# Quest-style attention and a capacity-limited expert layer: keys and queries loaded as token-major rows of 256 B, and turned, reduced and cast in thirds

## The chip, the core and the metric

The kernel runs on one core of one Trainium2 chip. Its time is the device time of one execution in microseconds (us). A core has five engines that run side by side, each through its own instructions in order: TensorE (PE in the profile, its weight loads PEld), VectorE (DVE), ScalarE (ACT), GpSimd (POOL), and SyncE (SP), which here only issues DMA transfers. A name with a q at its end (SPq, POOLq) is the part of an engine that issues transfers and waits.

## What is computed

```python
q, k, v: (4, 8, 768, 64)                     # batch, heads, tokens, width; float32
k_chunks = k.reshape(B, H, 24, 32, D)        # 24 chunks of 32 tokens
k_min, k_max = np.min(k_chunks, axis=3), np.max(k_chunks, axis=3)
ub = np.sum(np.maximum(q * k_min, q * k_max), axis=-1)     # bound per query and chunk
ub = np.where(causal, ub, -1e9)
top_chunks = np.argsort(ub, axis=-1)[..., -6:]             # the 6 best chunks per query
scores = scale * np.matmul(q, k.transpose(0, 1, 3, 2))     # masked to these and to the causal part
attn_out = softmax(scores) @ v
x = attn_out.transpose(0, 2, 1, 3).reshape(3072, 512)      # then the expert layer
logits = x @ w_gate; expert_idx = argmax(logits); gate_w = probability of that expert
# per expert the 80 tokens with the largest gate_w:
out[tok_idx] = gate_w[tok_idx, None] * (np.maximum(x[tok_idx] @ w1[e], 0) @ w2[e])
```

## The kernel before

The 32 pairs of batch and head are taken as 8 quads of 4 heads. On the 128 partitions lie 4 heads by 32. A quad has three query blocks of 256 tokens (THIRD = 256), and these have 1, 2 and 3 pairs of key blocks, so a quad is 6 rounds and the attention is 48 rounds, in the loop at lines 815 to 883 (rd is the round, g its quad, r its place in the quad).

For a quad, `load_k` and `load_q` (line 218) bring 768 KB each into one buffer each, kn and qn: partition (head, t) holds 24 rows of 64 floats. With the view of lines 186 and 187 the token is 24 t + c, so the 24 rows of a partition lie one behind another in memory, 6 KB. `load_v` (line 232) is four loads of 192 KB, whose rows are 64 floats, 256 B.

`prep(g)` (line 239) takes the tiles of a quad and returns its steps. K (line 256): VectorE turns blocks of 32 x 32 from kn to kT (line 253; in quad 0 in two halves, else in one instruction of 1536 columns), GpSimd casts kT to KB, VectorE takes the minimum and the maximum of each chunk (lines 261, 262), GpSimd subtracts them (line 263). Q (line 266): VectorE turns qn to qT, ScalarE takes relu into qp, GpSimd casts to QB. `bound` (line 276) is 80 small matmuls into ps_u, which takes the four banks that the scores use too; VectorE turns them into ub (line 295), and the banks are free again. `rank` and `unselect` make the mask from ub. kT, qT, qp, ub, kn and qn have one buffer each, so the next quad's data can come in only when the last reader is done.

A round is: scores on TensorE (`score`), exponentials on ScalarE (line 358, tile E), a causal cut on GpSimd for some (line 362), and one round later `value` and `denom` on TensorE. After a query block, `scales` and `rows` normalize: TensorE transposes into a pool of two banks (ps_dT, ps_xn), VectorE makes den, rec, lg_h (lines 421 to 428) and x_nat (line 443). After the second quad of a batch (odd g) `gates` follows: a chain on VectorE with lg, mx, sh (line 462), an exponential ex on ScalarE (line 465), and gmask (line 488). `merge` (line 510) turns gmask on TensorE (ps_g, line 515), ScalarE copies it to cand, and VectorE alternates MAX8 and MATCH_REPLACE8 on it (lines 522, 524) to keep the 80 best per expert. After the rounds come the gathers and the experts' two matmuls.

The order on TensorE and SP is the order of the program (line 799). On VectorE, ScalarE and GpSimd a planner puts the instructions in order before the run, by its own costs and by due times that it works out backwards from the users; on the chip each engine keeps that order. In the loop, the K step of quad g+1 stands at r = 0 of quad g, the Q step at r = 1, `bound` behind the values of r = 3; the loads of quad g+2 stand at r = 3, behind the v loads of r = 1 and in front of zero fills of the output (line 131) and stores of x (line 449) in SP's queue. Since K and Q wait only for their data and buffers, the planner puts them up to a quad ahead. Weights come by GpSimd's queue (line 145).

Of the kernel before, what the change touches and what calls it, by code (L numbers as in the profile page):

```python
# [35 lines left out]
def kernel(  # L36
# [146 lines left out]
    slotrhs = big.tile([P, TBLK, 6, NEXP], BF16, name="slotrhs")  # L183
    cand = [big.tile([P, CAP + SEQ], F32, name=f"cand_{s}") for s in range(2)]

    q4 = q.rearrange("b h (t c) d -> (b h t) c d", t=CHUNK)
    k4 = k.rearrange("b h (t c) d -> (b h t) c d", t=CHUNK)
    v4 = v.rearrange("b h (c p) d -> p (b h c) d", p=P)
    x_dram_v = x_dram.rearrange("(c p) d -> p c d", p=P)

# [8 lines left out]
    with tc.tile_pool(name="small", bufs=2) as small, \  # L199
# [18 lines left out]
        def load(g, src, name, parts=1):  # L218
            dst = qkp.tile([P, NCHUNK, HEAD_D], F32, name=name)
            n = NCHUNK // parts  # L220
            for i in range(parts):
                nc.sync.dma_start(out=dst[:, n * i:n * (i + 1), :],
                                  in_=src[P * g:P * (g + 1), n * i:n * (i + 1), :])
            nats[(g, name)] = dst

        def load_k(g, parts=1):
            load(g, k4, "kn", parts)
# [8 lines left out]
                                  in_=v4[:, 24 * g + 6 * h:24 * g + 6 * (h + 1), :])  # L236
            nats[(g, "vn")] = dst

        def prep(g, parts=1):
            s = g % 2  # L240
            qn, kn = nats[(g, "qn")], nats[(g, "kn")]
            kT = qfp.tile([P, 2, SEQ], F32, name="kT")
            qT = qfp.tile([P, 2, SEQ], F32, name="qT")
            qp = qfp.tile([P, 2, SEQ - P], F32, name="qp")
            kmx = small.tile([P, 2, NCHUNK], F32, name="kmx")
            spare["kT"], spare["qT"], spare["qp"] = kT[:], qT[:], qp[:]

            def turn(dst, src):
                n = NCHUNK // parts
                view = dst[:].rearrange("p f (t c) -> p c f t", c=NCHUNK)  # L250
                for i in range(parts):
                    cs = slice(n * i, n * (i + 1))
                    nc.vector.transpose(out=view[:, cs],  # L253
                                        in_=src[:, cs, :].rearrange("p c (f d) -> p c f d", f=2))

            def keys():
                turn(kT, kn)
                nc.gpsimd.tensor_copy(out=KB[s][:], in_=kT[:])
                kv = kT[:].rearrange("p f (c t) -> p f c t", t=CHUNK)
                lo = KMM[s][:, 0, :, 0:NCHUNK]  # L260
                nc.vector.tensor_reduce(out=lo, in_=kv, axis=mybir.AxisListType.X, op=ALU.min)
                nc.vector.tensor_reduce(out=kmx[:], in_=kv, axis=mybir.AxisListType.X, op=ALU.max)  # L262
                nc.gpsimd.tensor_tensor(out=KMM[s][:, 1, :, 0:NCHUNK], in0=kmx[:], in1=lo,  # L263
                                        op=ALU.subtract)

            def queries():
                turn(qT, qn)
                nc.scalar.activation(out=qp[:], in_=qT[:, :, P:SEQ],  # L268
                                     func=mybir.ActivationFunctionType.Relu)
                nc.gpsimd.tensor_copy(out=QB[s][:], in_=qT[:])  # L270

            ub = rankp.tile([P, 5, 4, 32], F32, name="ub")
            top8 = rankp.tile([P, 5, 4, 8], F32, name="top8")
            spare["ub"], spare["top8"] = ub[:], top8[:]

            def bound():
                ps_u = [psS.tile([P, 5, 32], F32, space=bass.MemoryType.PSUM, tag="ps_S",
                                 name="ps_u") for _ in range(4)]
                part = lambda x, lo: x[:, lo:].rearrange("p (i j t) -> p i j t", i=5, t=32)
                for w in range(3):  # L280
                    for f in range(1 if w == 0 else 2):
                        for j in range(4):
                            for h in range(4):
                                rs = slice(32 * h, 32 * (h + 1))
                                if w == 0:
                                    lhsT, rhs = later[rs, :], part(ind, P)
                                elif w == 1:
                                    lhsT, rhs = KMM[s][rs, 0, f, :], part(qT[:, f, :], P)
                                else:
                                    lhsT, rhs = KMM[s][rs, 1, f, :], part(qp[:, f, :], 0)  # L290
                                nc.tensor.matmul(out=ps_u[h][32 * j:32 * (j + 1), :, :], lhsT=lhsT,  # L291
                                                 rhs=rhs[rs, :, j, :], start=(w == 0),
                                                 stop=(w == 2 and f == 1), skip_group_check=True)
                for h in range(4):
                    nc.vector.transpose(out=ub[:, :, h, :], in_=ps_u[h][:])  # L295

            def rank():
                for j in range(5):
                    for h in range(4):
                        nc.vector.max(out=top8[:, j, h, :], in_=ub[:, j, h, 0:NCHUNK])  # L300
                nc.vector.tensor_tensor(out=PEN[s][:, :, :, 0:NCHUNK], in0=ub[:, :, :, 0:NCHUNK],
                                        in1=top8[:, :, :, 5:6].to_broadcast([P, 5, 4, NCHUNK]),
                                        op=ALU.is_lt)

            def unselect():
                ps_pen = misc([P, 5 * P], BF16, "ps_pen")
                for j in range(5):
                    nc.tensor.transpose(ps_pen[:, j * P:(j + 1) * P],
                                        PEN[s][:, j].rearrange("p h c -> p (h c)"), ident_bf[:])
                nc.scalar.activation(out=PENT[s][:], in_=ps_pen[:],  # L310
                                     func=mybir.ActivationFunctionType.Copy)

            return {"K": keys, "Q": queries, "bound": bound, "rank": rank, "unselect": unselect}

        rounds = []
        for g in range(NQUAD):
# [480 lines left out]
        stages = 0  # L797
        FREEZE = N - 6
        with tc.manual_schedule(engines={mybir.EngineType.PE, mybir.EngineType.SP}):
            load_k(0, 2)  # L800
            load_q(0, 2)
            nc.sync.dma_start(out=wg_sb[:], in_=moe_w_gate.rearrange("(t r) e -> r t e", r=P))
            load_v(0)
            load_k(1)
            load_q(1)
            load_v(1)
            u = prep(0, 2)
            for step in ("K", "Q", "bound", "rank", "unselect"):
                u[step]()
            nc.vector.memset(cand[0][0:NEXP, 0:CAP], 0.0)  # L810
            build_projection()
            build_selection()
# [2 lines left out]
            for rd in range(N + 1):  # L815
                g, r = divmod(rd, 6)
                before, after = [], []
                if r == 0 and g + 1 < NQUAD:
                    u = prep(g + 1)
                if rd - 4 in ends:  # L820
                    before.append(lambda e=ends[rd - 4]: rows(*e))
                if rd - 3 in ends:
                    before.append(lambda e=ends[rd - 3]: scales(*e))
                if g + 1 < NQUAD:
                    if r == 0:
                        before.append(u["K"])
                    elif r == 1:
                        before.append(u["Q"])
                    elif r == 4:
                        before.insert(0, u["rank"])  # L830
                    elif r == 5:
# [155 lines left out]
```

## Time and profile before

| what | value |
|---|---|
| two runs | 424.32 and 422.92 us, median 423.62 us |
| profiled execution | 419.83 us, of which 418.0 us from the first to the last instruction (the span) |
| TensorE busy (matmuls) | 280.4 us (67%) |
| VectorE busy | 255.8 us (61%) |
| ScalarE busy | 143.6 us (34%) |
| GpSimd busy | 124.9 us (30%) |
| mean granted TensorE clock | 0.846 of full speed |

A busy share is a mean over stages with different limits. Which engine sets the end of a stage is read from the waits and the timeline of that stage. A wait names the instruction that waited and the one that came last of those it waited for. The granted clock has two levels, 1.2 GHz (0.50 of full speed) and 2.4 GHz (1.00); a number between is a mean.

### The profile page before, as it was taken

To read this page: it belongs to the slowest core of one execution; us is meant where nothing else is said; L and a number is where in the kernel's file an instruction comes from. 1 tells how busy PE (TensorE), PEld (TensorE's weight loads), DVE (VectorE), ACT (ScalarE), POOL (GpSimd) and SP (SyncE) were. 2 spreads that over 40 slices of the span, in tenths; PEclk is the share of its full clock that TensorE was granted. 3 is DMA by queue.
4 is the path that set the end of the run, shared out by engine and by line. 5 is a ranking of instruction groups with operands and counts; after the bars stand their busy time and mean duration, and the time that the engine had idled before them with its cause. 6 is when DMAs were issued, how large, how long until landed. Compare 5 with 4: busy or idle time off the path is not lost. (4 is left out here: it accounts for less than half of the span.)

```text
span 418.0 us, 12461 instructions
## 1 busy us (share of the span) xinstructions
PE 280.4 (67%) x5330; PEld 173.1 (41%) x5330; DVE 255.8 (61%) x686; ACT 143.6 (34%) x322; POOL 124.9 (30%) x289
## 2 busy tenths in 40 slices
PE   0319799189735896399383990897579988435882
PEld 0214565055423453255151550554346644233661
DVE  6996630874279974781499928759893672621331
ACT  1116364045501362236222450454224452601220
POOL 3633061026400231216301510363315320151221
PEclk9957999769968699589977997699689998755997
DMA  9542019463993079175990291719748900011111
GB/s 238 172 120 78 4 26 262 145 101 104 234 245 129 2 133 286 29 162 115 290 225 4 30 243 60 104 46 182 115 91 155 176 29 27 25 39 26 48 34 40
DMA packets 48328, 47.82 MB, mean 114 GB/s; under 512 B 26918, under 2 KB 38310, under 8 KB 48272
## 3 DMA queue, kind: packets, MB, share of 16 engines
q0 software_dynamic: 13536, 18.67, 26.5%
q1 hardware_dynamic: 34736, 28.35, 23.1%
q8 instruction: 42, 0.69, 0.7%
q14 instruction: 14, 0.11, 0.1%
HBM read 53.10 MB, written 10.76 MB: 153 GB/s over the span
## 5 line engine op out<-in xcount | busy, mean ns | idle before, releaser
L358 ACT ACTIVATE E<-ps_S 128x384 f32<-128x384 f32 (+1 forms) x192 | 88.9, 547 | 67.0 <-PE ps_S L351 65.9
L375 PE MATMUL ps_num<-E,vn 128*32 128x256 f32 (+1 forms) x1536 | 99.2, 378 | 0.0
L362 POOL TENSOR_SCALAR_AFFINE_SELECT E<-E 128x256 f32<-128x256 f32 x96 | 40.6, 446 | 109.8 <-ACT E L358 109.8
L375 PEld LDWEIGHTS ps_num<-E,vn 128*32 128x32 f32 x1536 | 52.4, 116 | 32.8 <-issue 9.6
L391 PE MATMUL ps_den<-E,ones 128*32 128x256 f32 (+1 forms) x768 | 54.1, 370 | 5.9 <-ACT DSB L409 5.9
L347 PE MATMUL ps_S<-QB,KB 32*128 32x256 bf16 (+1 forms) x768 | 42.0, 276 | 21.0 <-DVE ub L295 17.1
L253 DVE STREAM_TRANSPOSE kT<-kn 128x1536 f32<-128x1536 f32 (+1 forms) x9 | 32.1, 3589 | 32.5 <-DMA kn<-in_k_dram 32.5
L253 DVE STREAM_TRANSPOSE qT<-qn 128x1536 f32<-128x1536 f32 (+1 forms) x9 | 32.1, 3569 | 11.5 <-PE ps_u L291 8.9
L291 PE MATMUL ps_u<-ind,later 32*32 32x160 bf16 x128 | 6.0, 270 | 46.7 <-ACT E L358 32.2
L391 PEld LDWEIGHTS ps_den<-E,ones 128*32 128x32 f32 x768 | 25.8, 114 | 24.7 <-ACT DSB L409 10.9
L522 DVE MAX8 cand<-cand 8x8 f32<-8x848 f32 (+2 forms) x40 | 33.2, 830 | 4.5 <-ACT cand L516 3.8
L347 PEld LDWEIGHTS <-KB 32*128 32x128 bf16 x768 | 20.3, 97 | 36.2 <-issue 32.2
L421 DVE TENSOR_REDUCE den<-ps_dT 128x4 f32<-128x8 f32 x48 | 5.8, 155 | 43.9 <-PE ps_dT L417 43.9
L268 ACT ACTIVATE qp<-qT 128x1280 f32<-128x1280 f32 x8 | 10.2, 1270 | 57.5 <-DVE qT L253 46.2
L524 DVE MATCH_REPLACE8 cand<-cand,cand 8x848 f32<-8x848 f32 (+2 forms) x36 | 29.4, 818 | 0.0
L351 PE MATMUL ps_S<-PENT,ind 32*128 32x256 bf16 (+1 forms) x384 | 27.1, 271 | 0.4 <-ACT PENT L310 0.2
L443 DVE TENSOR_TENSOR x_nat<-ps_xn,rec 128x512 bf16<-128x512 f32 x24 | 16.2, 675 | 15.1 <-PE ps_xn L442 15.1
L465 ACT ACTIVATE ex<-sh 128x16 f32<-128x16 f32 x12 | 2.6, 215 | 60.6 <-DVE sh L462 60.6
L291 PEld LDWEIGHTS <-later 32*32 32x32 bf16 x128 | 2.4, 91 | 50.5 <-issue 36.2
L263 POOL TENSOR_TENSOR KMM<-kmx,KMM 128x48 f32<-128x48 f32 x8 | 2.6, 326 | 59.7 <-DVE kmx L262 59.7
L398 ACT ACTIVATE npt<-ps_num 128x512 f32<-128x512 f32 x24 | 14.7, 614 | 9.5 <-PE ps_num L375 9.5
L515 PE MATMUL ps_g<-ident_f,gmask 128*8 128x128 f32 x18 | 3.7, 314 | 21.2 <-DVE gmask L488 20.5
(208 smaller groups left out, 450.5 us busy)
## 6 DMA issues: line engine op xcount, KB each, us to landing
w<-in_moe_w_dram POOLq DMA_DIRECT2D x11, 1024.0 KB, 9.5
vn<-in_v_dram SPq DMA_DIRECT2D x32, 192.0 KB, 7.2
out_dram<-zero_tile SPq DMA_DIRECT2D x12, 512.0 KB, 6.9
kn<-in_k_dram SPq DMA_DIRECT2D x7, 768.0 KB, 6.5
qn<-in_q_dram SPq DMA_DIRECT2D x7, 768.0 KB, 6.9
x_dram<-x_nat SPq DMA_DIRECT2D x12, 257.0 KB, 2.9
kn<-in_k_dram SPq DMA_DIRECT2D x2, 384.0 KB, 3.5
qn<-in_q_dram SPq DMA_DIRECT2D x2, 384.0 KB, 4.9
```

The source lines that it names most:

```text
L253: nc.vector.transpose(out=view[:, cs], in_=src[:, cs, :].rearrange("p c (f d) -> p c f d", f=2))
L268: nc.scalar.activation(out=qp[:], in_=qT[:, :, P:SEQ], func=mybir.ActivationFunctionType.Relu)
L347: nc.tensor.matmul(out=ps_S[h][:, m, 0:wid], lhsT=KB[s][rs, w, keys], rhs=QB[s][rs, w, q0:q0 + wid], start=(w == 0), stop=False, skip_grou ...
L351: nc.tensor.matmul(out=ps_S[h][:, m, lo - q0:wid], lhsT=ind[rs, keys], rhs=PENT[s][rs, lo - P:q0 + wid - P], start=False, stop=True, skip_ ...
L358: nc.scalar.activation(out=E[:].rearrange("p m q -> p (m q)")[:, 0:last], in_=ps_S[h][:].rearrange("p m q -> p (m q)")[:, 0:last], func=my ...
L362: nc.gpsimd.affine_select(out=E[:, :, 0:P], in_=E[:, :, 0:P], compare_op=ALU.is_ge, fill=0.0, base=0, pattern=[[0, 2], [1, P]], channel_mu ...
L375: nc.tensor.matmul(out=NUM[q0:q0 + 32, a, c0:THIRD], lhsT=nats[(g, "vn")][:, kb, 2 * a + r, 32 * f:32 * (f + 1)], rhs=Es[rd][2 * a + r][:, ...
L391: nc.tensor.matmul(out=dn[q0:q0 + 32, c0:THIRD], lhsT=ones32[:, a, :], rhs=Es[rd][2 * a + r][:, m, 0:wid], start=(i == 0 and x == 0), stop ...
L398: nc.scalar.activation(out=npt[:], in_=NUM[:], func=mybir.ActivationFunctionType.Copy)
L443: nc.vector.tensor_tensor(out=xbuf[(b, t)][:, :, P * gi:P * (gi + 1)].bitcast(BF16).rearrange("p j (k d) -> p j k d", d=HEAD_D), in0=ps_xn ...
L522: nc.vector.max(out=top, in_=src[:, 0:w])
L524: nc.vector.match_replace(out=src[:, 0:w], in_to_replace=top, in_values=src[:, 0:w], imm_value=-2.0)
```

## The change

Keys and queries are loaded so that partition (head, t) holds token 32 c + t: rows of 64 floats, 256 B, that lie 8 KB apart in memory. A load is now one per head, onto 32 partitions; in quad 0 each is also cut into three by chunks, so keys and queries of quad 0 are 24 loads instead of 4, those of every other quad 8 instead of 2. The turn writes rows of 32 floats side by side (before, each float of such a row lay 24 floats from the last). Turn, cast, the two extremes, the subtraction and relu work on a third (8 chunks, 256 tokens) at a time; K and Q are now lists of three steps. `prep(g+2)` is called at r = 5 of quad g, one round sooner; its steps stand where they stood.

```diff
-    q4 = q.rearrange("b h (t c) d -> (b h t) c d", t=CHUNK)
-    k4 = k.rearrange("b h (t c) d -> (b h t) c d", t=CHUNK)
+    q4 = q.rearrange("b h (c t) d -> (b h) t c d", t=CHUNK)
+    k4 = k.rearrange("b h (c t) d -> (b h) t c d", t=CHUNK)
...
             for i in range(parts):
-                nc.sync.dma_start(out=dst[:, n * i:n * (i + 1), :],
-                                  in_=src[P * g:P * (g + 1), n * i:n * (i + 1), :])
+                for h in range(4):
+                    nc.sync.dma_start(out=dst[32 * h:32 * (h + 1), n * i:n * (i + 1), :],
+                                      in_=src[4 * g + h, :, n * i:n * (i + 1), :])
...
-            def turn(dst, src):
-                n = NCHUNK // parts
-                view = dst[:].rearrange("p f (t c) -> p c f t", c=NCHUNK)
-                for i in range(parts):
-                    cs = slice(n * i, n * (i + 1))
-                    nc.vector.transpose(out=view[:, cs],
-                                        in_=src[:, cs, :].rearrange("p c (f d) -> p c f d", f=2))
-
-            def keys():
-                turn(kT, kn)
-                nc.gpsimd.tensor_copy(out=KB[s][:], in_=kT[:])
-                kv = kT[:].rearrange("p f (c t) -> p f c t", t=CHUNK)
-                lo = KMM[s][:, 0, :, 0:NCHUNK]
+            def turn(dst, src, i):
+                cs, ts = slice(8 * i, 8 * (i + 1)), slice(THIRD * i, THIRD * (i + 1))
+                nc.vector.transpose(
+                    out=dst[:, :, ts].rearrange("p f (c t) -> p c f t", t=CHUNK),
+                    in_=src[:, cs, :].rearrange("p c (f d) -> p c f d", f=2))
+                return cs, ts
+
+            def keys(i):
+                cs, ts = turn(kT, kn, i)
+                nc.gpsimd.tensor_copy(out=KB[s][:, :, ts], in_=kT[:, :, ts])
+                kv = kT[:, :, ts].rearrange("p f (c t) -> p f c t", t=CHUNK)
+                lo = KMM[s][:, 0, :, cs]
                 nc.vector.tensor_reduce(out=lo, in_=kv, axis=mybir.AxisListType.X, op=ALU.min)
-                nc.vector.tensor_reduce(out=kmx[:], in_=kv, axis=mybir.AxisListType.X, op=ALU.max)
-                nc.gpsimd.tensor_tensor(out=KMM[s][:, 1, :, 0:NCHUNK], in0=kmx[:], in1=lo,
+                nc.vector.tensor_reduce(out=kmx[:, :, cs], in_=kv, axis=mybir.AxisListType.X,
+                                        op=ALU.max)
+                nc.gpsimd.tensor_tensor(out=KMM[s][:, 1, :, cs], in0=kmx[:, :, cs], in1=lo,
                                         op=ALU.subtract)
...
-            def queries():
-                turn(qT, qn)
-                nc.scalar.activation(out=qp[:], in_=qT[:, :, P:SEQ],
+            def queries(i):
+                cs, ts = turn(qT, qn, i)
+                lo = max(THIRD * i, P)
+                nc.scalar.activation(out=qp[:, :, lo - P:ts.stop - P], in_=qT[:, :, lo:ts.stop],
                                      func=mybir.ActivationFunctionType.Relu)
-                nc.gpsimd.tensor_copy(out=QB[s][:], in_=qT[:])
+                nc.gpsimd.tensor_copy(out=QB[s][:, :, ts], in_=qT[:, :, ts])
...
-            load_k(0, 2)
-            load_q(0, 2)
+            load_k(0, 3)
+            load_q(0, 3)
...
+                if r == 5 and g + 2 < NQUAD or rd == 0:
+                    nxt = prep(g + 2 if rd else 1)
                 if r == 0 and g + 1 < NQUAD:
-                    u = prep(g + 1)
+                    u = nxt
...
                     if r == 0:
-                        before.append(u["K"])
+                        before += u["K"]
                     elif r == 1:
-                        before.append(u["Q"])
+                        before += u["Q"]
```

## Rows read from the trace of the kernel before

**Rows 1.** The page's first line: the span.
```profile
span 418.0 us, 12461 instructions
```
**Rows 2.** Windows: stretch in us, its length, busy us per engine, PEclk, DMA, GB/s.
```profile
72.00:92.00 20.00, 9.34 (x223) 5.96 (x223) 14.75 (x21) 3.12 (x7) 2.91 (x10) 0.66 0.57 135
...
112.00:137.00 25.00, 11.26 (x248) 6.98 (x249) 19.68 (x22) 4.16 (x11) 3.39 (x10) 0.77 0.70 196
```
**Rows 3.** Waits, whole run: who waited for whom, us in total, times, longest.
```profile
PE ps_u L291 <- ACT E L358: 32.2, 11, 10.2
...
DVE kT L253 <- DMA kn<-in_k_dram: 32.5, 6, 6.2
...
PE ps_g L515 <- DVE gmask L488: 20.5, 3, 7.5
...
PE ps_S L347 <- DVE ub L295: 17.1, 6, 7.1
```
**Rows 4.** Timeline, 67 to 92: start, us, engine, line, out<-in, [idle before <-releaser].
```profile
67.72 0.85 SPq L222 DMA_DIRECT2D kn<-in_k_dram  x1
...
74.25 4.01 DVE L253 STREAM_TRANSPOSE kT<-kn 128x1536 f32<-128x1536 f32 x1 [5.94 <-DMA kn<-in_k_dram]
...
81.62 0.68 DVE L443 TENSOR_TENSOR x_nat<-ps_xn,rec 128x512 bf16<-128x512 f32 x1
...
83.60 0.17 DVE L462 TENSOR_TENSOR sh<-lg,mx 128x16 f32<-128x16 f32 x1
...
84.56 0.29 PE L291 MATMUL ps_u<-ind,later 32*32 32x160 bf16 x1 [10.10 <-ACT E L358]
...
91.34 1.04 DVE L295 STREAM_TRANSPOSE ub<-ps_u 128x160 f32<-128x160 f32 x4
```
**Rows 5.** Timeline, 117 to 138, VectorE and TensorE.
```profile
117.26 4.01 DVE L253 STREAM_TRANSPOSE kT<-kn 128x1536 f32<-128x1536 f32 x1 [6.20 <-DMA kn<-in_k_dram]
121.05 0.23 DVE L488 TENSOR_TENSOR gmask<-oh,x_nat 128x16 f32<-128x16 bf16 x1
...
132.64 3.98 DVE L253 STREAM_TRANSPOSE qT<-qn 128x1536 f32<-128x1536 f32 x1
...
137.47 1.01 DVE L295 STREAM_TRANSPOSE ub<-ps_u 128x160 f32<-128x160 f32 x4
...
137.84 1.27 PE L347 MATMUL ps_S<-QB,KB 32*128 32x256 bf16 x8 [4.79 <-DVE ub L295]
```
**Rows 6.** Groups by line and shape: xcount | busy us, mean ns | idle before.
```profile
L253 DVE STREAM_TRANSPOSE kT<-kn 128x1536 f32<-128x1536 f32 x7 | 28.1, 4012 | 29.8 <-DMA kn<-in_k_dram 29.8
...
L261 DVE TENSOR_REDUCE KMM<-kT 128x48 f32<-128x1536 f32 x8 | 14.0, 1753 | 0.3
...
L295 DVE STREAM_TRANSPOSE ub<-ps_u 128x160 f32<-128x160 f32 x32 | 8.3, 312 | 0.0
...
L253 DVE STREAM_TRANSPOSE kT<-kn 128x768 f32<-128x768 f32 x2 | 4.0, 2110 | 2.7 <-DMA kn<-in_k_dram 2.7
...
L460 DVE TENSOR_REDUCE mx<-lg 128x2 f32<-128x16 f32 x12 | 2.0, 167 | 0.3
```
**Rows 7.** Windows near the start, columns as in rows 2; GB/s last.
```profile
3.00:5.00 2.00, 0.00 (x0) 0.00 (x0) 0.99 (x1) 0.00 (x0) 1.81 (x8) 1.00 1.03 402
8.00:10.00 2.00, 0.00 (x0) 0.00 (x0) 1.97 (x3) 0.00 (x0) 0.00 (x0) 1.00 1.31 220
```
**Rows 8.** Timeline of the start and the first quad, several engines.
```profile
0.80 0.87 SPq L222 DMA_DIRECT2D kn<-in_k_dram  x2
...
4.01 4.01 DVE L253 STREAM_TRANSPOSE kT<-kn 128x768 f32<-128x768 f32 x2 [2.73 <-DMA kn<-in_k_dram]
...
26.60 4.00 DVE L253 STREAM_TRANSPOSE qT<-qn 128x1536 f32<-128x1536 f32 x1
...
31.81 1.61 ACT L358 ACTIVATE E<-ps_S 128x384 f32<-128x384 f32 x4
...
50.60 1.06 PE L347 MATMUL ps_S<-QB,KB 32*128 32x256 bf16 x8 [1.90 <-DVE ub L295]
```

More of the change, by code (lines that the diff above doesn't have):

```diff
@@ L237, in load_v, with prep @@
             nats[(g, "vn")] = dst
-        def prep(g, parts=1):
+        def prep(g):
             s = g % 2
@@ L311, in unselect @@
                                      func=mybir.ActivationFunctionType.Copy)
-            return {"K": keys, "Q": queries, "bound": bound, "rank": rank, "unselect": unselect}
+            return {"K": [lambda i=i: keys(i) for i in range(3)],
+                    "Q": [lambda i=i: queries(i) for i in range(3)],                     "bound": bound, "rank": rank, "unselect": unselect}
         rounds = []
@@ L806 @@
             load_v(1)
-            u = prep(0, 2)
-            for step in ("K", "Q", "bound", "rank", "unselect"):
-                u[step]()
+            u = prep(0)
+            for step in u["K"] + u["Q"] + [u["bound"], u["rank"], u["unselect"]]:
+                step()
             nc.vector.memset(cand[0][0:NEXP, 0:CAP], 0.0)
```

## The prediction

> **What bounds the kernel now.** The span is 418.0 us [rows 1]. I read the stretches first. Of the eight quads, the ones in the middle alternate between a stretch in which TensorE is busy nearly throughout and a stretch in which it is busy less than half of the time: 9.34 of 20 us from 72 to 92, and 11.26 of 25 us from 112 to 137. In those two the engine with the most work is VectorE (14.75 and 19.68 us), and TensorE's granted clock is down to a mean of 0.66 and 0.77 of full speed [rows 2]. So neither engine is full; something is waited for.
>
> The view of waits says what. TensorE waits 32.2 us for exponentials before the bound (ps_u), 20.5 us for gmask and 17.1 us for ub; VectorE itself waits 32.5 us in six places for the keys' load [rows 3]. The timeline joins them. In the odd kind of stretch (near 74, 163 and 252) the keys of a later quad are asked for at 67.72 and VectorE, which takes its instructions in order, sits until they land at 74.25. It then turns them, takes the two extremes, and only at 81.62 comes to x_nat, and at 83.60 to sh. ScalarE's queue stands behind sh, so TensorE goes on at 84.56, after 10.10 us of nothing. The bound's ub comes at 91.34 [rows 4]. In the even kind with a merge (near 117 and 206) the turn starts at 117.26 and gmask follows at 121.05. From there VectorE goes on to the extremes, merge steps and the turn of the queries (3.98 us, from 132.64), and reaches ub at 137.47. TensorE waits for gmask and again 4.79 us for ub [rows 5]. The end of each stretch is thus set by: the keys' landing, then VectorE's work up to ub. At the start VectorE is full as well: the first exponentials (31.81) come right behind the turn of quad 1's queries (from 26.60) [rows 8].
>
> **The turns.** A turn of 1536 columns takes 4.012 us, one of 768 takes 2.110: 2.48 ns a column and 0.2 us fixed [rows 6]. The change writes rows of 32 floats without a step of 24. The nearest row is the turn of ub, which writes such rows: 0.312 us for 160 columns, so at most 1.95 ns a column, and 1.0 if 0.15 us is fixed [rows 6]. A reduction reads 1536 columns in 1.753 us and 16 in 0.167, which is 1.04 ns a column and 0.15 fixed [rows 6]. So I take 0.15 + 512 x 1.04 ns = 0.69 us for a third of a turn; upper bound 1.4 us if nothing is gained (2.48 ns), lower bound 0.5 us with nothing fixed. Neighbours overlap a little: the keys' turn and two extremes are 4.01 + 1.75 + 1.75 = 7.51 us by their durations and take 7.37, from 74.25 to 81.62 [rows 4, 6]. With 0.05 us an instruction off, the nine key steps are 9 x 0.64 = 5.8 us, though six of them are extremes, which alone get 0.3 us dearer; the queries' 4.0 us become 1.9. Saved per quad: 1.6 us at the keys, 2.0 at the queries.
>
> **The loads.** Long rows move at 402 GB/s from 3 to 5 us. From 8 to 10 us, when rows of 256 B (v) move, it is 220 [rows 7]. A load of 768 KB (786 thousand bytes) thus takes 3.6 us and not 2.0: keys land 1.6 us later, queries, behind them in the same queue, 3.2 us later. Lower bound: nothing, if other transfers set the landing; upper bound below, among the rivals. SP issues eight loads for two; issuing takes some 0.44 us each (two take 0.87) [rows 8], which in the steady state goes on while earlier rows move. Queued behind them on SP are zero fills and x_dram stores, which nobody waits for before the experts' gather. The query loads have a quad's time to land, so their delay is hidden; that cover goes if the quad gets more than 10 us shorter.
>
> **Casts and relu in thirds** add fixed parts on GpSimd and ScalarE. GpSimd's KB and QB casts and the small subtraction are wanted a quad later; ScalarE's relu goes from one to three instructions; if each new one costs 0.2 us fixed, as on VectorE's turn, that is 0.4 us a quad beside VectorE's turn. I count nothing; without that cover it would be 8 x 0.4 = 3 us. The earlier prep call issues no instruction by itself; it moves where tiles are taken, so it can only reorder.
>
> **The sum, by place.**
> Start: 24 loads at 0.44 us put the last query load of quad 0 out at 0.8 + 24 x 0.44 = 11.4 us. The first one now is issued at 0.80 and used at 4.01, 3.2 later [rows 8]; so these land by 14.6, and v, which follows, starts to move near 14. Then v, keys and queries of quad 1, 2.36 MB at 220 GB/s, land about 24.7. Three thirds of a turn (1.9) and the last relu (about 0.6) end at 27.2; first exponentials then instead of 31.81: -4.6. If the planner keeps quad 1's keys ahead of ub as now, VectorE waits for them and the gain is lost (+0.7). I take -4.6, since the planner too sees 24 issues ahead of those keys.
> First quad: the ub stall of 1.90 us at 50.60 [rows 8] is as short as what the query turn saves: -1.9.
> Odd stretches, three: keys land 1.6 later and take 1.6 less: 0. Ub comes 2.0 earlier, but TensorE is busy until shortly before it: -0.2 each, -0.6.
> Even stretches, two: again 0 at the keys. Gmask now lies between the turn and the extremes, so its due time in the plan lies between theirs. A third's turn has less work behind it (0.7 for 1.75 us), so it is due later, and gmask goes first; TensorE then reaches the bound earlier, and ub gets ahead of the query steps and one merge step. From 132.64 to 137.47 that is 4.8 us [rows 5]: -4.8 each, -9.6; if the order stays, -2.0 each; at most the 7 us by which TensorE now waits for gmask more.
> Sum: -4.6 - 1.9 - 0.6 - 9.6 = -16.7. The span becomes 401.3 us, the profiled execution (419.83, 1.83 around the span) 403.1. The two runs shown have a median of 423.62, 3.8 above the profiled one; with that difference kept, 406.9.
>
> **Rivals.**
> A, better order everywhere. If the key steps also go behind x_nat and sh in the odd stretches, the 10.10 us go. Ub then waits for keys (75.8 + 5.8) and queries (1.9) and comes at 83.5 instead of 91.34: 8 us each, 24 in three. With 6 in each even stretch and the start: -4.6 - 1.9 - 24 - 12 = -42.5, 381. For it: a third leaves VectorE free after 0.7 us. Against: in [rows 4] all three key instructions went ahead of x_nat.
> B, the loads eat the gain. Five stretches start at the keys' landing [rows 3, 4, 5]. Without any delay the sum would be 16.7 + 5 x 1.6 = 24.7, and each us of delay costs 5. Keys landing 4.9 us later make it no change, 423.6, and 3.3 to 6.4 us make it 415.5 to 431; with weights, v and zero fills in the same bursts that is possible.
> C, slower. Each new load writes 32 partitions. No row shows such a load. If a quarter of the partitions takes only half the rate, 110 GB/s, 768 KB last 7.1 us: keys land 5.2 later, five times, 26 against the 20.1 gained in the steady state (24.7 less 4.6); and quad 1's queries land at 3 + (4 x 0.786 + 0.786 x 0.5) / 0.11 = 35 us, first exponentials 36.4, +4.6 instead of -4.6. Together +10.5: 434. It decides from a landing about 6 us later on. Against it: the four quarters follow one another in one queue, and may overlap.
> The Trainium skill, page SBUF — State Buffer, section Door 1: The DMA port swizzle, speaks for C: a transfer's rate goes by how many of the 16 ports its partitions reach, and 32 neighbouring partitions reach eight. By its figure of 436 GB/s half is 218, which is the rate of the short rows already, and then the rule would cost nothing; only if the halving comes on top is it C.
> D, the turns get no faster (2.48 ns a column stays, 3 x 1.4 us a turn). Then the keys' delay of 1.6 us and 0.3 us more for the extremes stand five times, 9.5, against what the order gives in the even stretches (2 x 2.8, without the saved 2.0) and the start: no change to speak of, within B's bounds, and its chance is in B's.
>
> **Numbers.** Likeliest, 406.9, its own range 399 to 415: 0.44. A 0.24, B 0.20, C 0.12. Faster by over 2% (below 415.2; 2% is about what a measurement of this kernel tells from no change): 0.68. Within 2%: 0.20. Slower: 0.12. For 8 in 10: from 384, leaving 0.08 of A below, to 428, leaving C above.
>
> **What would show it.** Turn thirds near 0.69 us; key loads landing 1 to 3 us later than the 6.5 us after issue that they take now; TensorE's wait for ub near nothing, its wait for gmask gone, its wait for exponentials before ps_u still about 30 us. Wrong: turn thirds above 1 us; keys landing over 5 us later; VectorE standing before quad 1's keys ahead of the first ub; a new wait for the queries' load.

## The result: 376.7 us, a gain almost three times the forecast

The changed kernel took 376.68 us (two executions, 374.09 and 379.28) against 423.62: ratio 0.889 with an interval of 0.862 to 0.916. Measured again in more rounds beside the experiments it was 0.893 (0.886 to 0.900). The gain is 45 to 47 us; 16.7 were forecast, and the time lies outside the range. It is close to rival A's 381. The experiments ran on more than one chip, and the kernel before took 415.6 to 421.8 us on them. So experiments are compared by their ratio to the kernel before on the same chip, and a difference of ratios is turned into us with 421.7.

The profiled execution's span fell from 418.0 to 377.6 us. The page's span line and busy times of after:

```profile
span 377.6 us, 12675 instructions
...
PE 275.4 (73%) x5330; PEld 167.9 (44%) x5330; DVE 224.6 (59%) x748; ACT 145.0 (38%) x338; POOL 131.5 (35%) x337
```

TensorE is busy 5 us less for the same 5330 matmuls: it stands still less, and its mean granted clock is 0.897 instead of 0.846. The other 35 us are time in which it stood. The view of waits of after (who waited for whom, us in total, times, longest) answers [rows 3]:

```profile
PE ps_u L293 <- DVE qT L251: 15.4, 5, 7.6
...
PE ps_u L293 <- ACT E L361: 11.7, 21, 2.1
...
PE ps_g L518 <- DVE gmask L491: 10.3, 1, 10.3
...
PE ps_S L350 <- DVE ub L297: 4.5, 2, 2.5
...
DVE kT L251 <- DMA kn<-in_k_dram: 5.6, 2, 3.2
```

TensorE's wait for exponentials before the bound is 11.7 us in 21 short pieces instead of 32.2 in which three were 10 us each; gmask 10.3 once instead of 20.5 in three places; ub 4.5 instead of 17.1. VectorE waits 5.6 us for keys, all in the first 25 us, instead of 32.5. The wait for qT has grown, from 1.6 us to 15.4. TensorE's rows of it, and of the wait in front of it in the start, first before, then after:

```profile
14.29 0.36 PE L291 MATMUL ps_u<-ind,later 32*32 32x160 bf16 x16 [14.29 <-DVE later L79]
16.28 1.74 PE L291 MATMUL ps_u<-qT,KMM 32*32 32x160 f32 x64 [1.63 <-DVE qT L253]
```

```profile
7.26 0.36 PE L293 MATMUL ps_u<-ind,later 32*32 32x160 bf16 x16 [7.26 <-DVE later L79]
15.28 1.55 PE L293 MATMUL ps_u<-qT,KMM 32*32 32x160 f32 x53 [7.64 <-DVE qT L251]
...
182.96 1.52 PE L293 MATMUL ps_u<-qT,KMM 32*32 32x160 f32 x51 [6.23 <-DVE qT L251]
```

The 7.64 us in the start are no new wait: quad 0's bound stood 14.29 and 1.63 us before and stands 7.26 and 7.64 now, and its queries come at about the same time. New are the 6.23 us at 182.96 and 1.5 us in three short pieces.

The timeline of after, VectorE's rows around the bound of the third quad, answers [rows 4]:

```profile
50.77 0.69 DVE L446 TENSOR_TENSOR x_nat<-ps_xn,rec 128x512 bf16<-128x512 f32 x1 [3.29 <-PE ps_xn L445]
51.37 1.29 DVE L251 STREAM_TRANSPOSE kT<-kn 128x512 f32<-128x512 f32 x2
...
54.93 0.70 DVE L251 STREAM_TRANSPOSE kT<-kn 128x512 f32<-128x512 f32 x1
...
62.86 0.69 DVE L446 TENSOR_TENSOR x_nat<-ps_xn,rec 128x512 bf16<-128x512 f32 x1 [3.60 <-PE ps_xn L445]
...
64.85 0.17 DVE L465 TENSOR_TENSOR sh<-lg,mx 128x16 f32<-128x16 f32 x1
...
66.00 1.90 DVE L251 STREAM_TRANSPOSE qT<-qn 128x512 f32<-128x512 f32 x3
...
72.38 1.04 DVE L297 STREAM_TRANSPOSE ub<-ps_u 128x160 f32<-128x160 f32 x4 [4.48 <-PE ps_u L293]
```

Read the order, not the lengths. The keys turned at 51.37 are those of the quad whose ub comes at 72.38, and their load was issued at 28.54: they have lain ready for long. In the kernel before, the keys turned at 74.25 and the queries turned just ahead of the ub at 91.34 belong to the quad after that ub [rows 4]. VectorE worked one quad further ahead there, and so it stood before loads that had only just been asked for, with x_nat, sh and TensorE behind it. In after, VectorE comes to sh at 64.85 with nothing in its way.

### The profile page after: what moved, and what is told of

It reads as the page before. It is cut to its first block, busy times and chain, and to the rows that moved or that the text cites. A ratio compares the mean times of both kernels' runs of the same rounds, so it can differ in the third digit from the quotient of the medians.

```text
span 377.6 us, 12675 instructions
## 1 busy us (share of the span) xinstructions
PE 275.4 (73%) x5330; PEld 167.9 (44%) x5330; DVE 224.6 (59%) x748; ACT 145.0 (38%) x338; POOL 131.5 (35%) x337
## 5 line engine op out<-in xcount | busy, mean ns | idle before, releaser
L394 PE MATMUL ps_den<-E,ones 128*32 128x256 f32 (+1 forms) x768 | 55.5, 378 | 6.1 <-ACT DSB L412 6.0
L350 PE MATMUL ps_S<-QB,KB 32*128 32x256 bf16 (+1 forms) x768 | 37.8, 270 | 8.2 <-DVE ub L297 4.5
L525 DVE MAX8 cand<-cand 8x8 f32<-8x848 f32 (+2 forms) x40 | 33.1, 828 | 11.1 <-ACT cand L519 10.5
L350 PEld LDWEIGHTS <-KB 32*128 32x128 bf16 x768 | 17.6, 96 | 21.5 <-issue 18.8
L354 PE MATMUL ps_S<-PENT,ind 32*128 32x256 bf16 (+1 forms) x384 | 25.9, 263 | 0.4 <-ACT PENT L312 0.2
L293 PE MATMUL ps_u<-qT,KMM 32*32 32x160 f32 x512 | 11.3, 366 | 15.4 <-DVE qT L251 15.4
L270 ACT ACTIVATE qp<-qT 128x512 f32<-128x512 f32 (+1 forms) x24 | 12.5, 568 | 22.6 <-DVE qT L251 22.6
L293 PE MATMUL ps_u<-ind,later 32*32 32x160 bf16 x128 | 6.7, 251 | 19.2 <-ACT E L361 11.7
L272 POOL CAST QB<-qT 128x512 bf16<-128x512 f32 x24 | 14.2, 610 | 17.4 <-DVE qT L251 17.4
L258 POOL CAST KB<-kT 128x512 bf16<-128x512 f32 x24 | 14.5, 609 | 15.9 <-DVE kT L251 15.9
L251 DVE STREAM_TRANSPOSE kT<-kn 128x512 f32<-128x512 f32 x24 | 16.0, 690 | 5.6 <-DMA kn<-in_k_dram 5.6
L293 PE MATMUL ps_u<-qp,KMM 32*32 32x160 f32 x512 | 13.3, 366 | 5.4 <-issue 5.4
## 6 DMA issues: line engine op xcount, KB each, us to landing
qn<-in_q_dram SPq DMA_DIRECT2D x28, 192.0 KB, 11.8
```

What stands on the lines that cost most here:

```text
L251: nc.vector.transpose(out=dst[:, :, ts].rearrange("p f (c t) -> p c f t", t=CHUNK), in_=src[:, cs, :].rearrange("p c (f d) -> p c f d", f=2))
L350: nc.tensor.matmul(out=ps_S[h][:, m, 0:wid], lhsT=KB[s][rs, w, keys], rhs=QB[s][rs, w, q0:q0 + wid], start=(w == 0), stop=False, skip_grou ...
L354: nc.tensor.matmul(out=ps_S[h][:, m, lo - q0:wid], lhsT=ind[rs, keys], rhs=PENT[s][rs, lo - P:q0 + wid - P], start=False, stop=True, skip_ ...
L394: nc.tensor.matmul(out=dn[q0:q0 + 32, c0:THIRD], lhsT=ones32[:, a, :], rhs=Es[rd][2 * a + r][:, m, 0:wid], start=(i == 0 and x == 0), stop ...
L525: nc.vector.max(out=top, in_=src[:, 0:w])
```

## The experiments

Each ratio is to the kernel before, with its 95% interval.

| run | loads | turn | K and Q steps | VectorE's order | ratio |
|---|---|---|---|---|---|
| e1_order_alone | long rows | step of 24 | whole | behind ub, the queries right behind the keys | 1.000 (0.996 to 1.005) |
| e5_order_late_queries | long rows | step of 24 | whole | as after | 0.944 (0.937 to 0.951) |
| e13_slow_whole_turn | short rows | step of 24 | whole | as after | 0.925 (0.919 to 0.931) |
| e2_slow_turn | short rows | step of 8 | thirds | as after | 0.915 (0.909 to 0.921) |
| e9_old_order_fast_turn | long rows | contiguous | whole | as before | 0.934 (0.928 to 0.941) |
| e3_long_rows | long rows | contiguous | thirds | as before | 0.934 (0.930 to 0.937) |
| e10_long_rows_four_loads | long rows, by head | contiguous | whole | between | 0.883 (0.876 to 0.889) |
| e6_long_rows_new_order | long rows | contiguous | whole | as after | 0.875 (0.869 to 0.882) |
| e4_whole_steps | short rows | contiguous | whole | as after | 0.876 (0.873 to 0.880) |
| e8_changed_again | short rows | contiguous | thirds | after itself | 0.893 (0.886 to 0.900) |

In all but e1 and e5 quad 0 is turned and reduced in thirds; in e13 these thirds have a step of 8. In e5 and e6 quad 1's keys still go ahead of the first ub; the rest of the order of keys, queries and ub is that of after. In e2, e3, e6, e9, e10 and e13 the tokens stand in another order than the later steps assume, with instructions of the same shapes. No run takes back the call of `prep` one round sooner; e3 and e9 have it together with the old order, so it does not bring the new order by itself.

### The order alone

```diff
-                    nc.vector.transpose(out=view[:, cs], in_=...)
+                    ins = nc.vector.transpose(out=view[:, cs], in_=...)
+                    if g > 1:
+                        tc.keep_in_program_order(ins)
```

> The kernel before, with two added statements: the turns of quad 2 and later are pinned, in VectorE's queue, behind the instruction that the program puts ahead of them. Loads in long rows, whole turns with a step of 24, whole extremes: all as before. With it VectorE turns a quad's keys after the ub, gates and x_nat of the quad before, and its queries after the keys, instead of ahead of them. Theory (the order alone carries most of the gain): the three stalls of about 10 us and the stalls behind gmask go, about 30 to 40 us of the 46.9; time 384 to 398. Rival (the faster turns carry it): at most 5 us off, 418 or more.

Ratio 1.000 (423.01 us beside 421.83): the theory missed, and so did its reason. The timeline of e1, one place of five:

```profile
64.94 4.00 DVE L253 STREAM_TRANSPOSE qT<-qn 128x1536 f32<-128x1536 f32 x1
...
68.97 1.27 ACT L271 ACTIVATE qp<-qT 128x1280 f32<-128x1280 f32 x1 [7.30 <-DVE qT L253]
...
72.02 1.51 PE L394 MATMUL ps_den<-E,ones 128*32 128x256 f32 x16 [6.95 <-ACT DSB L412]
```

The 10 us stalls were gone (the wait for exponentials before ps_u fell from 32.2 to 5.0 us), but the queries' turn had moved straight behind the keys. Their relu (qp) had a place in ScalarE's queue in the middle of a round's exponentials; it stood 7.30 us for the turn, everything on ScalarE behind it stood too, and TensorE lost 6.95 us. The five such waits are most of 30.5 us, where the kernel before has 5.9; TensorE's waits for GpSimd's masks of E add 12.2. One stall had been swapped for others. The next run moves the queries' step as well:

```diff
-                    elif r == 1:
+                    elif r == 3:
                         before.append(u["Q"])
```

> The kernel before, with the same two pinning statements as the run with the order alone, and the queries' step two rounds later in the program (at r = 3, ahead of the bound). So VectorE turns the queries behind the gates, right ahead of the bound, as the changed kernel does, and ScalarE's relu stands there too, and no longer ahead of a round's exponentials while the turn is still running. Loads in long rows and whole turns with a step of 24 stay. Theory (order is the main cause, and the run with the order alone only put the queries in the wrong place): 384 to 398. Rival (without the faster turn no order helps): 415 or more.

Ratio 0.944 (399.94 us), 24 us off, just above the range given. So the order alone is worth about half of the gain, but only with the queries in the right place. What is left shows in the timeline of e5, on TensorE:

```profile
64.79 1.35 PE L378 MATMUL ps_num<-E,vn 128*32 128x256 f32 x24 [1.54 <-POOL E L365]
...
78.85 1.74 PE L294 MATMUL ps_u<-qT,KMM 32*32 32x160 f32 x64 [2.40 <-DVE qT L253]
...
118.20 1.74 PE L294 MATMUL ps_u<-qT,KMM 32*32 32x160 f32 x64 [6.27 <-DVE qT L253]
```

The bound now waits for the slow turn of the queries right ahead of it, and GpSimd's masks of E wait behind a cast that waits for the slow turn of the keys.

### The loads and the order

```diff
-                for h in range(4):
-                    nc.sync.dma_start(out=dst[32 * h:32 * (h + 1), n * i:n * (i + 1), :],
-                                      in_=src[4 * g + h, :, n * i:n * (i + 1), :])
+                nc.sync.dma_start(out=dst[:, n * i:n * (i + 1), :],
+                                  in_=src[P * g:P * (g + 1), n * i:n * (i + 1), :])
```

> The changed kernel with the loads of before: whole tiles by one DMA each, rows of 6 KB (output not the reference's, since the tokens land elsewhere than the turn expects). Turns stay fast and in thirds, extremes, casts and relu in thirds. VectorE's order is that of the kernel before again, keys and queries of a quad ahead of the ub before them. Theory (the slower loads move the order, by landing later in the plan): the odd and even stalls come back, shortened by the faster turns: 395 to 412. Rival (order is set by the thirds or does not matter, and loads in short rows cost time): as fast as the changed kernel or faster, 377 or less.

Ratio 0.934 (393.49 us, just under the range of the theory): 17 us more than the changed kernel's 0.893, from nothing but the old loads. The timeline of e3, the same stretch as [rows 4], shows the old pattern in little:

```profile
64.86 1.31 DVE L250 STREAM_TRANSPOSE kT<-kn 128x512 f32<-128x512 f32 x2 [5.12 <-DMA kn<-in_k_dram]
...
68.43 0.70 DVE L250 STREAM_TRANSPOSE kT<-kn 128x512 f32<-128x512 f32 x1
...
69.06 0.65 DVE L445 TENSOR_TENSOR x_nat<-ps_xn,rec 128x512 bf16<-128x512 f32 x1
...
71.89 0.17 DVE L464 TENSOR_TENSOR sh<-lg,mx 128x16 f32<-128x16 f32 x1
...
72.85 0.29 PE L292 MATMUL ps_u<-ind,later 32*32 32x160 bf16 x1 [6.95 <-ACT E L360]
```

With the old loads the key steps stand ahead of x_nat and sh again and wait for the landing; the faster turn shortens the stall from 10.10 to 6.95 us and does not remove it. Since only the loads differ from after, it is they that moved VectorE's order. Whether it is by the landing that the planner counts on (many short rows, four issues) is argued, not shown; but the two runs with whole steps and long rows point the same way. e9 has one load, e10 four of one head each:

> The run with long rows in the new order, without its pins and with the queries' step back at r = 1: fast whole turns, long rows, and VectorE's order of the kernel before (a quad's keys and queries ahead of the ub before them). Output not the reference's (tokens land elsewhere). Against that run (368.3) only the order differs, with a fast turn; against the kernel before the fast turn and quad 0's thirds differ, in the old order. Theory (the order costs 15 to 25 us with the fast turn as well): 384 to 394. Rival (with the fast turn the order matters no longer): 366 to 374.

> As the run before it in this call (fast whole turns, long rows, nothing pinned), with each load issued as four of 32 partitions, one per head. Output not the reference's. VectorE's order lies between the two: queries behind ub, keys in part ahead of it. It tells what the number of loads does without short rows. Theory (order decides, a load of 32 partitions costs no transfer time that matters): between the old order's and the new order's time, 370 to 386. Rival (loads of 32 partitions move at half the rate and hold the keys back): 390 or more.

e9 gave 0.934, as expected, e10 0.883, with the queries behind ub and the keys still ahead of it, but behind x_nat and sh. VectorE's rows in e9's timeline, around the bound of the third quad:

```profile
67.29 1.78 DVE L252 STREAM_TRANSPOSE kT<-kn 128x1536 f32<-128x1536 f32 x1 [6.10 <-DMA kn<-in_k_dram]
...
72.43 0.68 DVE L447 TENSOR_TENSOR x_nat<-ps_xn,rec 128x512 bf16<-128x512 f32 x1
...
78.35 1.78 DVE L252 STREAM_TRANSPOSE qT<-qn 128x1536 f32<-128x1536 f32 x1 [2.62 <-POOL slotrhs L506]
...
80.05 1.00 DVE L298 STREAM_TRANSPOSE ub<-ps_u 128x160 f32<-128x160 f32 x4
```

The same stretch of e10:

```profile
61.70 0.69 DVE L448 TENSOR_TENSOR x_nat<-ps_xn,rec 128x512 bf16<-128x512 f32 x1 [3.61 <-PE ps_xn L447]
...
63.70 0.18 DVE L467 TENSOR_TENSOR sh<-lg,mx 128x16 f32<-128x16 f32 x1
...
68.61 1.78 DVE L253 STREAM_TRANSPOSE kT<-kn 128x1536 f32<-128x1536 f32 x1 [3.77 <-DMA kn<-in_k_dram]
...
73.75 1.03 DVE L299 STREAM_TRANSPOSE ub<-ps_u 128x160 f32<-128x160 f32 x4
```

In e10 VectorE still stands 3.77 us before the keys' load, but x_nat and sh are already through, so TensorE does not stand with it there. The time that the rival named did not come. The keys did land later, though: a quad's four loads took 10.2 us from the first issue to the last landing (median of seven quads), the one load of e3 5.4; what of it is due to the 32 partitions is not shown, for the v loads ahead of them were late too (9.0 us against 6.0). To see what the short rows cost by themselves, e6 has long rows with the new order pinned (`keep_in_program_order` on the turns, the queries' step at r = 3), whole steps, against e4 with short rows:

> The changed kernel in whole steps from quad 1 on (as in the run with whole steps), with loads in rows of 6 KB by one DMA each (output not the reference's: tokens land elsewhere), and the order of the changed kernel kept by pinning the turns and by the queries' step at r = 3. Against the run with whole steps (369.6) it differs in the loads alone, except in the start, where quad 1's keys go ahead of the first ub. Theory (the short rows cost nothing on the path by themselves, their only effect is the order): 364 to 372. Rival (the short rows hold keys and queries back): 350 to 361. A third reading, that the short rows help by more than the order: 378 or more.

Ratio 0.875 against e4's 0.876. Its first exponentials come at 27.40 us, e4's at 24.22, so up to 3 us of cost may hide in this tie, and the two intervals leave room for about 3 more. With e9 it also prices the order under a fast turn: 0.934 to 0.875, 25 us, about what e5 gains on the kernel before without one.

### The turn and the thirds

```diff
-                    out=dst[:, :, ts].rearrange("p f (c t) -> p c f t", t=CHUNK),
+                    out=dst[:, :, ts].rearrange("p f (t c) -> p c f t", t=CHUNK),
```

> The changed kernel with the turn's output written with a step of 24 floats again, in thirds (so the tokens stand in another order in kT and qT and the output is not the reference's). Loads, thirds and the order on every engine are those of the changed kernel, instruction for instruction. Theory (order): turn thirds 1.4 us, VectorE has room for most of it; about 2 us more in the start and up to 6 in the rest, 378 to 386. Rival (speed of the turn carries it): 6 x 0.7 us in each of eight quads lie on the path, 34 us, 400 to 412.

The expectation was wrong in its edit: within a third there are 8 chunks, so the step was 8 floats, and a third took 1.11 us, not 1.4. Ratio 0.915 (386.75 us, just above the range of the theory) against 0.893: 9 us, give or take 4, which is 56% of the 16.4 us by which VectorE is busier. In whole steps the step is 24:

```diff
     def turn(dst, src, i):
+        if g:
+            cs, ts = slice(0, NCHUNK), slice(0, SEQ)
...
-            "K": [lambda i=i: keys(i) for i in range(3)]
+            "K": [lambda i=i: keys(i) for i in range(1 if g else 3)]       # Q too
```

> The changed kernel, with keys and queries of quads 1 to 7 in one step each: one contiguous turn of 1536 columns, whole extremes, casts and relu; quad 0 stays in thirds, loads in rows of 256 B stay. Order of keys and queries against ub, gmask and x_nat as in the changed kernel. Theory (the loads moved the order, thirds did not): 375 to 382, a whole contiguous turn about 1.75 us. Rival (thirds let VectorE get to x_nat and gmask in time): 390 or more.

> The run with whole steps (369.6 beside a kernel before of 421.8), with the turn's output written with a step of 24 floats again: order on every engine and loads stay (tokens stand in another order, output not the reference's). Theory (a slow turn costs most when it is whole, since the bound, the relu and the cast wait for all 4 us of it: the waits for it, 15.8 us on TensorE and 9.4 by way of GpSimd, were the difference of the two runs with long rows): 390 to 400. Rival (as in thirds, where the slow turn cost about 9 us): 376 to 382.

The keys' turn in the groups by line and shape (xcount | busy us, mean ns | idle before), first in e4:

```profile
L253 DVE STREAM_TRANSPOSE kT<-kn 128x1536 f32<-128x1536 f32 x7 | 12.4, 1765 | 2.7 <-DMA kn<-in_k_dram 2.7
```

In e13:

```profile
L253 DVE STREAM_TRANSPOSE kT<-kn 128x1536 f32<-128x1536 f32 x7 | 27.9, 3992 | 2.2 <-DMA kn<-in_k_dram 2.2
```

In the changed kernel:

```profile
L251 DVE STREAM_TRANSPOSE kT<-kn 128x512 f32<-128x512 f32 x24 | 16.0, 690 | 5.6 <-DMA kn<-in_k_dram 5.6
```

e4 gave 0.876 (369.59 us), below the range of the theory and 7 us faster than the changed kernel: the thirds of quads 1 to 7 cost time. e13 gave 0.925 (384.04 us beside a kernel before of 415.63), 21 us more than e4; turned into us with 421.7 it is 390, the lower end of the theory's range. In both pairs (e2 and e8, e13 and e4) a slow turn costs 0.6 to 0.7 us for each us that VectorE is longer busy (e13: 14 turns by 2.23 us are 31), so there is no sign that thirds hide it. Where the thirds cost is shown by the timeline of the changed kernel in run e8:

```profile
99.98 0.42 ACT L270 ACTIVATE qp<-qT 128x256 f32<-128x256 f32 x1 [1.37 <-DVE qT L251]
...
100.30 0.58 ACT L361 ACTIVATE E<-ps_S 128x512 f32<-128x512 f32 x1
100.78 1.14 ACT L270 ACTIVATE qp<-qT 128x512 f32<-128x512 f32 x2
100.93 0.22 PE L293 MATMUL ps_u<-ind,later 32*32 32x160 bf16 x1 [1.41 <-ACT E L361]
...
101.81 1.07 ACT L361 ACTIVATE E<-ps_S 128x512 f32<-128x512 f32 x2
...
102.45 0.23 PE L293 MATMUL ps_u<-ind,later 32*32 32x160 bf16 x1 [1.30 <-ACT E L361]
```

The relu thirds stand between the exponentials, which must empty a bank each before the bound's matmuls may go on. Two runs take back single pieces:

```diff
-                nc.scalar.activation(out=qp[:, :, lo - P:ts.stop - P], in_=qT[:, :, lo:ts.stop], ...)
+                if i == 2:                                       # quads 1 to 7
+                    nc.scalar.activation(out=qp[:], in_=qT[:, :, P:SEQ], ...)
```

> The changed kernel (378.1 beside a kernel before of 421.6), with the relu of quads 1 to 7 in one instruction behind the third turn; turns, extremes and casts stay in thirds. Theory (the thirds cost 8.5 us because ScalarE runs relu thirds between the exponentials that TensorE waits for): 368 to 373. Rival (the smaller steps of VectorE and GpSimd cost it): 375 to 379.

> As the run before it in this call, with the two casts of quads 1 to 7 in one instruction each as well, behind the third turn. Theory (casts lie beside everything): within 2 us of the run before it. Rival (GpSimd's pieces hold back the masks of the exponentials): 3 to 6 us faster than it.

e14 gave 0.880 (0.875 to 0.885), e15 0.883 (0.879 to 0.888). The relu explains most of the 7 us (5.6 of them, each known to some 3.5 us), and TensorE's wait for exponentials before the bound fell from 11.8 to 6.4 us; the casts explain nothing that can be told.

### Beyond the change

In e4 the longest stall left is 9.97 us for gmask at 246.86: merge steps and the last quad's keys stand ahead of the gates.

```diff
-                nc.vector.max(out=top, in_=src[:, 0:w])
+                tc.keep_in_program_order(nc.vector.max(out=top, in_=src[:, 0:w]))
```

> The changed kernel in whole steps from quad 1 on, and the merge's MAX8 steps pinned behind what the program puts ahead of them, so that gates, the queries' turn and ub go ahead of merge steps. The stalls of 9.97 us (gmask), 6.11 us (queries' turn) and 2 x 2 us (ub) of the run with whole steps should go: theory 352 to 362. Rival (VectorE has no room there, and the merge comes late for what follows it): 367 or more.

Ratio 0.858 (0.854 to 0.863), 7 us less than e4. The stalls got shorter and did not go: the one for gmask is 5.39 us now, the one for qT near 173 us 3.30 instead of 6.11, and ub keeps one of 3.00. Then the start, where SP issues 24 loads at 0.49 us each:

```diff
-            load_k(0, 3)
-            load_q(0, 3)
+            load_k(0, 1)      # e12: 2
+            load_q(0, 1)      # e12: 2
```

> The run with the merge pinned (362.1), with quad 0's keys and queries loaded whole, four loads each in place of twelve; turns stay in thirds. Theory (the start is held by the issuing of 24 loads at 0.49 us): the last query third is turned 3 to 4 us earlier than at 14.6, 357 to 360. Rival (the transfers hold it, or VectorE before the first ub): 361.5 to 364.

> As the run before it, with quad 0's keys and queries in two loads per head, 16 in all. Theory (issuing holds the start): the last query third 2 to 3 us earlier, 358.5 to 361. Rival: 361.5 to 364.

e11 0.852 (0.847 to 0.858), e12 0.849 (0.842 to 0.856); the two can't be told apart, and e11 not from e7 either. In e11 the theory's sign failed: the queries are through at 14.5 us (14.9 in e7), and the first keys, which now come as whole loads, are turned at 7.11 us instead of 4.71. So the issuing is not all that holds the start. SP's rows and the turn of quad 0's queries in e12:

```profile
0.80 3.98 SPq L223 DMA_DIRECT2D kn<-in_k_dram  x8
4.83 4.06 SPq L223 DMA_DIRECT2D qn<-in_q_dram  x8
...
10.87 1.89 DVE L253 STREAM_TRANSPOSE qT<-qn 128x512 f32<-128x512 f32 x3
```

The queries are through at 12.8 us instead of the 14.9 of e7, and the first exponentials come at 21.63 instead of 23.74. e12 (whole steps, merge pinned, 16 loads in the start) takes 352.7 us beside 417.2, a ratio 5% below the changed kernel's; 2 us of that are the start.

## Why the prediction was wrong, point by point

The gain in steps along the table, each in us of 421.7: the order, 0.944, -24; quad 0's thirds with the short rows, 0.944 to 0.925 (e5, e13), -8; the contiguous turn, 0.925 to 0.876 (e13, e4), -21; the thirds, 0.876 to 0.893 (e4, e8), +7. Together -45. Each step is known to 3 or 4 us, and taken in another order the steps might share the gain otherwise. The -8 lies in the start: first exponentials at 31.82 in e5, 23.93 in e13.

**The turn's price was right**: 0.69 us a third forecast, 0.690 and 0.679 measured.

**The sum without the loads' delay was right, for the old order.** It was 24.7 us; e3, which has the fast turn, the thirds and the old loads and order, gained 28. In part that is luck, for the pieces are off both ways: TensorE's stalls in the odd stretches shrank by 11.1 us (5.4 in that sum), those for gmask and ub in the two even ones by 7.1 (12.8), and the first exponentials came 6.9 sooner (4.6).

**The start was right in direction and too small**: -4.6 forecast; first exponentials at 24.10 instead of 31.81, -7.7. The last query third came when forecast (turned at 14.51). What failed here was to leave quad 1's query turn ahead of the first exponentials; it comes at 36.93 now, behind them.

**The first quad** was right in its size: the 1.90 us stall is gone. The saved turn was not needed for it: in e5, which has the slow turn and the new order, it is gone too.

**The odd stretches are the step that failed**: "keys land 1.6 later and take 1.6 less: 0". Measured: three stalls, 10.10, 10.23 and 10.17 us, have gone. The step kept the key steps where they stood in the old plan, at the landing and ahead of x_nat and sh. But the change alters the loads, and with later loads the plan itself comes out otherwise: key steps behind ub and x_nat, a quad's keys turned long after they landed. The same assumption lay under the late landing's price of 5 us for each us of delay: nobody waits for that landing any more. One of the signs that the prediction named shows it: the wait for exponentials before ps_u, which was to stay at about 30 us, is 11.7. The delay of the keys was about as small as forecast: a quad's four loads take 7.4 us from the first issue to the last landing (median of seven quads, by the landings in the trace) and the one load took 6.5, so 0.9 us more where 1.6 was forecast. The queries' loads take 15.8 instead of 6.9, where 3.2 later was forecast; why so long stays open, and past the start no engine waits for them.

**The even stretches**: -9.6 by gmask and ub going ahead of key and query steps. In size that came at the two places meant: TensorE's long waits there were 26.3 us (7.48 and 6.83 for gmask, 4.79 and 7.15 for ub) and are 14.1 (5.44 without a named wait at 111.52, 6.23 for qT at 182.96, 2.47 for ub), 12 us less. But the reason was another. The thirds were to send gmask ahead; e4 has no thirds there and no wait for gmask at these two places either, and e3, with thirds and the old loads, still waits 5.31 and 4.02 us for it. It is the new order of the keys again, and that the number fits is luck. At a third place, which the sum left out, gmask stands 10.34 us instead of 6.15 behind merge steps. The next quad's query turn, which was to go behind ub, now comes a quad later, right ahead of the bound that needs it: that is the new wait for qT, 6.23 us at 182.96.

**Relu and casts in thirds at nothing**: wrong for the relu. That it lies "beside VectorE's turn" held for its busy time, but in ScalarE's queue it lies between exponentials; 7 us for all the thirds, most of it by the relu (e14).

**The rivals.** A's order was what happened in the odd stretches, with the time nearly right (381). Its reason was not: it was argued from thirds, which leave VectorE free sooner, and e4 has the same order with whole steps. What I held against it, that all three key instructions went ahead of x_nat in [rows 4], was evidence from the very plan that the change replaces. B falls: short rows cost at most some 6 us by themselves (e4, e6), and no stretch starts at the keys' landing now. C falls: it needed 110 GB/s and keys 5.2 us later. While quad 1's loads move, each onto 32 partitions, windows of after (columns as in [rows 2], GB/s last) show 192 together with v's loads, and 177 from 19.3 to 24.2 us, when v's first four have landed (19.23) and the next are not yet issued (24.21):

```profile
16.00:24.00 8.00, 4.30 (x141) 2.77 (x123) 3.37 (x25) 0.70 (x1) 0.00 (x0) 1.00 1.11 192
19.30:24.20 4.90, 1.88 (x29) 1.08 (x29) 2.58 (x23) 0.80 (x2) 0.00 (x0) 1.00 1.00 177
```

The Trainium skill, page SBUF — State Buffer, section Door 1: The DMA port swizzle, says that a transfer's rate goes by the ports that its partitions reach. These rows show no further halving on top of the short rows' 220 GB/s [rows 7]. D falls with the turn's price.

What stays open: why the planner moves the steps (no run shows the costs that it reckons with), and a gap of 5.44 us on TensorE inside the bound at 111.52 that the profile puts down to no wait; e8 has it with 4.64, e4 with 1.05 and e14 with 0.79, so it shrinks when the relu is whole.

## What to carry to other kernels

Where a planner orders the engines' queues, a change in a load's shape can change the order of everything that uses the load: before summing durations, ask which steps would move, and do not take an order seen in the old trace for that of the new kernel. An instruction that is nearly free can cost its whole wait when it stands in the queue of an engine that others wait for, as the relu did here twice. Cut a step into parts only where something waits for its first part; in quad 0 the parts overlap the loads, in the other quads they cost 7 us.

## What the runs showed of the hardware

The time of VectorE's 32 x 32 turn depends on the step of its output: 1536 columns take 1.77 us with contiguous rows and 3.99 us with a step of 24 floats, and 512 columns take 0.69 us contiguous and 1.11 us with a step of 8.

How long loads take to land, from the page's issues (KB each, median us from issue to landing), first before, then after:

```profile
kn<-in_k_dram SPq DMA_DIRECT2D x7, 768.0 KB, 6.5
qn<-in_q_dram SPq DMA_DIRECT2D x7, 768.0 KB, 6.9
```

```profile
kn<-in_k_dram SPq DMA_DIRECT2D x28, 192.0 KB, 4.8
qn<-in_q_dram SPq DMA_DIRECT2D x28, 192.0 KB, 11.8
```

A load of 192 KB onto 32 partitions, with rows of 256 B, landed sooner than the whole load for the keys and later for the queries, so its own time says little: a quad's keys were complete 7.4 us after the first issue instead of 6.5, its queries 15.8 instead of 6.9. Issuing costs SP 0.49 us a load in the start.
